# FNet mixing and a cosine-gated MLP: tokens as pairs from folded real DFTs, the channel transform folded into the weights, integer phase rounding

## The chip, the cores and the metric

The kernel runs on one core of one Trainium2 chip. Times are device microseconds (us) from the first to the last instruction of an execution. Several executions are timed and the median is quoted. The engines are TensorE (PE in the profile, PEld for its weight loads), VectorE (DVE), ScalarE (ACT), GpSimd (POOL) and SyncE (SP, which here only issues DMAs). A "record" is one line of the trace: an instruction with its start and duration.

## The reference

```python
def _attn_ref(x):                    # x: (8, 3008, 256) float32
    X = np.fft.fft(x, axis=1)        # over the sequence: "s-DFT", 3008 points
    X = np.fft.fft(X, axis=2)        # over the channels: "d-transform", 256 points
    return X.real.astype(np.float32)

def _moe_ref(x, w_in, w_out):        # x: (24064, 256), w_in: (256, 2048), w_out: (2048, 256)
    h = x @ w_in
    g = h * np.cos(h)
    return (g @ w_out).astype(np.float32)
```

The output is `_moe_ref` of the flattened `_attn_ref`, all in float32.

## The kernel before

3008 is 47 times 64. Stage A does the 47-point factor of the s-DFT as matmuls with a 47-row operand and writes the result to a scratch tensor in DRAM, from which it is read back in another layout. Then six chunks of up to 512 tokens follow per batch: the second DFT factor (`BJ`), the d-transform (`CdS`), the first MLP matmul (`w1`), the phase chain, the second MLP matmul (`w2`).

```python
def emit_A(b, xts):                            # stage A
    zd = zdram_tile()                          # [94, 64 * 256] in DRAM
    for g in range(8):
        sa = stagA_tile()                      # [94, 2048]
        for q in range(4):
            n = 4 * g + q
            pa = pbig_tile()
            nc.tensor.matmul(pa, lhsT=LA, rhs=xts[:, n * 512 : (n + 1) * 512], start=True, stop=True)
            nc.vector.tensor_copy(out=sa[:, q * 512 : (q + 1) * 512], in_=pa[0:94, :])
        nc.sync.dma_start(out=zd[:, g * 2048 : (g + 1) * 2048], in_=sa)
    return zd
# ... emit_chunk: z2 loaded from zd, BJ matmuls, copies, CdS matmuls, copies; then per hidden slice f of 16:
    for cc in range(2):
        nc.tensor.matmul(pm[:, 0:ntok], lhsT=w1[cc][:, f * 128 : (f + 1) * 128], rhs=at[cc][:, 0:ntok],
                         start=(cc == 0), stop=(cc == 1))
    nc.scalar.activation(out=tt, in_=pm, func=AF.Copy, bias=BIG, scale=1.0)           # round to integer
    nc.vector.scalar_tensor_tensor(out=mm, in0=tt, scalar=-BIG, in1=pm, op0=ALU.add, op1=ALU.subtract)
    nc.scalar.activation(out=ss, in_=mm, func=AF.Sin, bias=0.0, scale=-math.pi)       # half angle
    nc.scalar.activation(out=qq, in_=ss, func=AF.Square, bias=0.0, scale=math.sqrt(2.0))
    nc.vector.scalar_tensor_tensor(out=gt, in0=qq, scalar=-1.0, in1=pm, op0=ALU.add, op1=ALU.mult)
    # ... four 128x256 matmuls of slice f - 2 with w2
```

(Shortened: slices of the tile widths and the loop over sub-blocks are left out.)

## Time and profile before

| | before |
|---|---|
| median | 4,835.48 us (4,835.38 to 4,835.50, 4 runs) |
| TensorE busy | 3,646 us, 75% |
| VectorE, ScalarE busy | 1,328 us, 1,523 us |
| mean granted TensorE clock | 0.876 |

The first lines of the page give each engine's busy time, then 40 equal slices of the span: a digit is the busy share in tenths, PEclk the clock granted to TensorE in tenths.

```profile
span 4834.8 us, 30926 instructions
PE 3645.8 (75%) x12000; PEld 2201.5 (46%) x12000; DVE 1328.4 (27%) x1985; ACT 1523.2 (32%) x2594; POOL 150.4 (3%) x196
PE   0408995499863998739977499666995579958998
PEclk9999995799966998769977799677996789959999
DMA  2101101111011010111001110011101021011100
```

An average of 75% hides two regimes: runs of 9 (TensorE is full) and pits. The windows view of five stretches of 30 us shows what they are. Its columns are the stretch, its length, busy us and instruction count of each engine, the granted clock, the mean busy share of the 16 DMA engines, and GB/s.

```profile
170.00:200.00 30.00, 14.38 (x16) 4.79 (x16) 5.32 (x8) 0.00 (x0) 0.00 (x0) 1.00 0.13 54
290.00:320.00 30.00, 0.00 (x0) 0.00 (x0) 0.00 (x0) 0.00 (x0) 0.00 (x0) 1.00 0.07 28
410.00:440.00 30.00, 30.00 (x107) 19.82 (x106) 12.20 (x18) 15.96 (x26) 0.00 (x0) 1.00 0.00 1
740.00:770.00 30.00, 14.38 (x16) 4.79 (x16) 5.32 (x8) 0.00 (x0) 0.00 (x0) 0.50 0.13 53
920.00:950.00 30.00, 0.00 (x0) 0.00 (x0) 0.00 (x0) 0.00 (x0) 0.00 (x0) 0.50 0.06 26
```

Stage A (170, 740) advances at the speed of scratch stores that keep 0.13 of the DMA engines busy, which is 2 of 16. The lower clock at 740 costs nothing: the stage does the same 16 matmul records in 30 us at 1.00 and at 0.50. At 290 and 920 nothing computes; one DMA engine of 16 (0.06 to 0.07) is loading. At 410 TensorE has no gap.

In the list of costliest groups (line, engine, operation, names, shapes, count, then busy us and mean ns, then idle time before it and what ended it) stage A is the matmul L153:

```profile
L153 PE MATMUL pbig<-xbig,LA 47*128 47x512 f32 x512 | 417.1, 982 | 535.6 <-DVE stagA L160 398.6
L160 DVE COPY stagA<-pbig 94x512 f32<-94x512 f32 x256 | 171.0, 685 | 770.7 <-DMA zdram<-stagA 492.5
```

417 us busy plus 536 us idle, and the waits view adds 612 us in which the first `BJ` matmul of a batch waits for the scratch reload (145 us once, 73 to 78 us six times, 17 us once). In all that is about 1,565 us; the rest, about 3,270 us, is TensorE almost without a gap. The timeline there (start, duration, records):

```profile
414.57 1.89 PE L227 MATMUL po<-w_78,gj 128*128 128x256 f32 x8
416.30 1.02 PE L238 MATMUL pm<-at,w_74 128*128 128x512 f32 x2
417.15 1.02 PE L238 MATMUL pm<-at,w_75 128*128 128x512 f32 x2
418.01 1.89 PE L227 MATMUL po<-w_78,gj 128*128 128x256 f32 x8
```

A float32 matmul leaves two records. From 414.57 to 418.01 one hidden slice takes 3.44 us; a 128x512 matmul takes 0.85 us from start to start, a 128x256 one 0.43 us. A record's duration (1.02 for two) is longer than the distance to the next start.

### The profile page before, as it was taken

The page shows a single profiled execution, that of the slowest core. Times are in us where ns is not written, and L with a number is a line of the kernel's source. Part 1 is how long each engine was busy: PE and PEld are TensorE (multiplying, and loading weights), DVE is VectorE, ACT ScalarE, POOL GpSimd, SP SyncE. Part 2 cuts the span into 40 slices and gives each one's busy share as a digit, 9 for nine tenths or more (in the row PEclk, how much of TensorE's full clock was granted, in tenths as well). Part 3 has the DMA queues.
Part 4 walks back from the last instruction along what each step waited for, and adds up shares of the span by engine and source line. Part 5 has one row for each costly group of instructions (what it writes and reads, how often), then busy time and mean ns, then how long its engine had stood idle before and what let it go on. Part 6 is the DMA issues. An engine that isn't in the chain of part 4 may idle for free.

```text
span 4834.8 us, 30926 instructions
## 1 busy us (share of the span) xinstructions
PE 3645.8 (75%) x12000; PEld 2201.5 (46%) x12000; DVE 1328.4 (27%) x1985; ACT 1523.2 (32%) x2594; POOL 150.4 (3%) x196
## 2 busy tenths in 40 slices
PE   0408995499863998739977499666995579958998
PEld 0105662266532664326633366334662356625665
DVE  0102331133321333213322133222332123323333
ACT  0003440144411543214422144122440234503444
POOL 0000000000000000000000000000000000000000
PEclk9999995799966998769977799677996789959999
DMA  2101101111011010111001110011101021011100
GB/s 87 46 31 42 26 6 54 37 33 26 15 50 51 14 26 24 45 47 27 16 29 45 39 27 17 37 40 36 26 17 45 36 43 22 9 53 33 27 17 9
DMA packets 109475, 158.33 MB, mean 33 GB/s; under 512 B 46057, under 2 KB 96280, under 8 KB 102552
## 3 DMA queue, kind: packets, MB, share of 16 engines
q1 hardware_dynamic: 59024, 131.04, 8.9%
q0 software_dynamic: 50304, 25.31, 2.5%
q8 instruction: 94, 1.54, 0.1%
q14 instruction: 53, 0.43, 0.0%
HBM read 81.75 MB, written 73.92 MB: 32 GB/s over the span
## 4 chain that ended last, share of the span: by engine, by line
issue 87%; another core or an unknown queue 5%; PE 3%; POOL 2%; DMA 2%; DVE 0%; ACT 0%; POOLq 0%; SPq 0%; DVEq 0%
POOL out_dram L294 2%; DMA zdram<-stagA 2%; PE po L227 1%; PE pm L238 1%; PE pbig L153 0%; PE pbig L210 0%; PE pbig L187 0%; DMA z_198<-zdram 0%; DVE stagA L160 0%; ACT tt L246 0%; DVE mm L250 0%; POOLq L294 0%; DVE gj L275 0%; ACT L259 0%
## 5 line engine op out<-in xcount | busy, mean ns | idle before, releaser
L227 PE MATMUL po<-w_78,gj 128*128 128x256 f32 (+1 forms) x6144 | 1471.7, 382 | 0.0
L227 PEld LDWEIGHTS po<-w_78,gj 128*128 128x128 f32 (+1 forms) x6144 | 1141.7, 188 | 491.5 <-issue 360.1
L153 PE MATMUL pbig<-xbig,LA 47*128 47x512 f32 x512 | 417.1, 982 | 535.6 <-DVE stagA L160 398.6
L238 PE MATMUL pm<-at,w_74 128*128 128x512 f32 (+1 forms) x1536 | 787.6, 594 | 28.9 <-DVE gj L275 28.9
L250 DVE SCALAR_TENSOR_TENSOR mm<-tt,pm 128x512 f32<-128x512 f32 (+1 forms) x768 | 519.4, 676 | 1004.5 <-ACT tt L246 1004.5
L238 PE MATMUL pm<-at,w_75 128*128 128x512 f32 (+1 forms) x1536 | 777.7, 588 | 0.0
L275 DVE SCALAR_TENSOR_TENSOR gj<-qq,pm 128x512 f32<-128x512 f32 (+1 forms) x768 | 519.2, 676 | 904.8 <-ACT qq L267 904.8
L218 ACT COPY at<-pbig 128x512 f32<-128x512 f32 (+1 forms) x96 | 55.3, 576 | 1962.0 <-PE pbig L210 1962.0
L246 ACT ACTIVATE tt<-pm 128x512 f32<-128x512 f32 (+1 forms) x768 | 450.7, 587 | 682.8 <-PE pm L238 682.8
L259 ACT ACTIVATE ss<-mm 128x512 f32<-128x512 f32 (+1 forms) x768 | 476.5, 620 | 545.0 <-DVE mm L250 545.0
L153 PEld LDWEIGHTS pbig<-xbig,LA 47*128 47x128 f32 x512 | 137.3, 286 | 804.6 <-DVE stagA L160 583.8
L267 ACT ACTIVATE qq<-ss 128x512 f32<-128x512 f32 (+1 forms) x768 | 476.2, 620 | 22.8
L238 PEld LDWEIGHTS pm<-at,w_75 128*128 128x128 f32 x1536 | 288.4, 190 | 362.9 <-issue 332.4
L160 DVE COPY stagA<-pbig 94x512 f32<-94x512 f32 x256 | 171.0, 685 | 770.7 <-DMA zdram<-stagA 492.5
L238 PEld LDWEIGHTS pm<-at,w_74 128*128 128x128 f32 x1536 | 279.5, 190 | 157.2 <-issue 84.3
L195 DVE COPY xt<-pbig 128x512 f32<-128x512 f32 x192 | 127.2, 677 | 788.9 <-PE pbig L187 788.9
L294 POOL DMA_DIRECT2D out_dram<-osb x192 | 150.2, 789 | 4675.2 <-ACT osb L293 4675.0
L210 PE MATMUL pbig<-xt,CdS_70 128*128 128x512 f32 (+1 forms) x384 | 181.2, 594 | 0.7
L210 PE MATMUL pbig<-xt,CdS_71 128*128 128x512 f32 (+1 forms) x384 | 177.0, 583 | 0.0
L187 PE MATMUL pbig<-BJ,z_198 128*128 128x128 f32 x32 | 6.7, 405 | 145.2 <-DMA z_198<-zdram 145.2
L210 PEld LDWEIGHTS pbig<-xt,CdS_71 128*128 128x128 f32 x384 | 73.0, 190 | 88.4 <-issue 88.4
L210 PEld LDWEIGHTS pbig<-xt,CdS_70 128*128 128x128 f32 x384 | 69.0, 190 | 70.9 <-issue 66.3
(103 smaller groups left out, 500.1 us busy)
## 6 DMA issues: line engine op xcount, KB each, us to landing
zdram<-stagA SPq DMA_DIRECT2D x64, 752.0 KB
out_dram<-osb POOLq DMA_DIRECT2D x184, 128.0 KB, 8.4
BJ<-fft_BJ SPq DMA_DIRECT2D x1, 3008.0 KB
w_78<-in_moe_w_out_dram SPq DMA_DIRECT2D x1, 2048.0 KB
w_74<-in_moe_w_in_dram SPq DMA_DIRECT2D x1, 1024.0 KB
w_75<-in_moe_w_in_dram SPq DMA_DIRECT2D x1, 1024.0 KB
z_198<-zdram SPq DMA_DIRECT2D x2, 512.0 KB
z_529<-zdram SPq DMA_DIRECT2D x2, 512.0 KB
```

Source lines behind the costliest of these rows:

```text
L153: nc.tensor.matmul(pa, lhsT=LA, rhs=xts[:, n * 512 : (n + 1) * 512], start=True, stop=True,)
L160: nc.vector.tensor_copy(out=sa[:, q * 512 : (q + 1) * 512], in_=pa[0:94, :])
L195: nc.vector.tensor_copy(out=xt[dch][:, 0 : 2 * ntok] .rearrange("p (hp j k) -> p j hp k", hp=2, j=nj)[:, 4 * g : 4 * g + ng, :, :], in_=pb ...
L210: nc.tensor.matmul(pd[:, 0:ntok], lhsT=CdS[dch][:, ri * 256 + cc * 128 : ri * 256 + cc * 128 + 128], rhs=xt[dch][:, ri * ntok : ri * ntok ...
L227: nc.tensor.matmul(pos[sub][0:nt, 0:ND], lhsT=gts[f][:, t0:t1], rhs=w2[:, f * ND : (f + 1) * ND], start=(f == 0), stop=(f == 15),)
L238: nc.tensor.matmul(pm[:, 0:ntok], lhsT=w1[cc][:, f * 128 : (f + 1) * 128], rhs=at[cc][:, 0:ntok], start=(cc == 0), stop=(cc == 1),)
L246: nc.scalar.activation(out=tt[:, 0:ntok], in_=pm[:, 0:ntok], func=AF.Copy, bias=BIG, scale=1.0)
L250: nc.vector.scalar_tensor_tensor(out=mm[:, 0:ntok], in0=tt[:, 0:ntok], scalar=-BIG, in1=pm[:, 0:ntok], op0=ALU.add, op1=ALU.subtract,)
L259: nc.scalar.activation(out=ss[:, 0:ntok], in_=mm[:, 0:ntok], func=AF.Sin, bias=0.0, scale=-math.pi,)
L267: nc.scalar.activation(out=qq[:, 0:ntok], in_=ss[:, 0:ntok], func=AF.Square, bias=0.0, scale=math.sqrt(2.0),)
L275: nc.vector.scalar_tensor_tensor(out=gt[:, 0:ntok], in0=qq[:, 0:ntok], scalar=-1.0, in1=pm[:, 0:ntok], op0=ALU.add, op1=ALU.mult,)
L294: nc.gpsimd.dma_start(out=out_r[b, 8 * c + t0 // 64 : 8 * c + t1 // 64, :, :], in_=ob[0:nt, :],)
```

## The change

The intent is to need fewer matmul columns and no large scratch tensor (a small one in DRAM stays, for one channel).

- For real input, the real output of token k is R - I and that of token -k is R + I (or the reverse), where R and I are the even and odd parts of the spectrum. So one product with R and one with I gives both tokens: h(k) = P + Q, h(-k) = P - Q, with P = Wc R and Q = Ws I.
- The d-transform is folded into `w_in` once at the start: Wc holds `w_in` combined with cosines, Ws with sines.
- The s-DFT is done on sequences folded twice (x(s) with x(-s), then with the half-length shift), as 24 matmuls of about 376 columns per batch, placed inside the stream of MLP steps. Channel 128 has no room in the 128 rows and goes as an "extra channel", for batches 1 to 7 together, from two DMAs that pick single 4-byte elements.
- The phase is rounded by writing int32 from ScalarE, and the sine is taken directly, which saves the squaring pass.

The stream has 376 steps (47 tiles of 256 token pairs, 8 steps each). The diff, cut to the core of the step (the folding, DFT, output rows and setup are left out):

```diff
-        for f in range(16):
-            pm = pm_tile()
-            for cc in range(2):
-                nc.tensor.matmul(pm[:, 0:ntok], lhsT=w1[cc][:, f * 128 : (f + 1) * 128], ...
+    def mlp1(T, s):                                  # TW = 256
+        for i in range(2):
+            nc.tensor.matmul(pp[:, i * TW : (i + 1) * TW], lhsT=Wc[:, f * 128 : (f + 1) * 128],
+                             rhs=Rr[:, pos : pos + TW], start=True, stop=True)
+        for i in range(2):
+            nc.tensor.matmul(pq[:, i * TW : (i + 1) * TW], lhsT=Ws[:, f * 128 : (f + 1) * 128],
+                             rhs=Ir[:, pos : pos + TW], start=True, stop=True)
+        for i in range(2):                           # extra channel
+            nc.vector.scalar_tensor_tensor(out=pt[...], in0=Rb[:, pos : pos + TW],
+                scalar=wex[:, f : f + 1], in1=pp[...], op0=ALU.mult, op1=ALU.add)
+        nc.vector.tensor_tensor(out=h[:, 0:512], in0=pt, in1=pq, op=ALU.add)
+        nc.vector.tensor_tensor(out=h[:, 512:1024]...[:, :, ::-1], in0=pt..., in1=pq..., op=ALU.subtract)
+        act_chain(h, 1024)
+    def act_chain(h, n):
+        nc.scalar.activation(out=k, in_=h[:, 0:n], func=AF.Copy, bias=0.25, scale=1.0)    # k is int32
+        nc.vector.tensor_tensor(out=r[:, 0:n], in0=h[:, 0:n], in1=k, op=ALU.subtract)
+        nc.scalar.activation(out=r[:, 0:n], in_=r[:, 0:n], func=AF.Sin, bias=halfpi, scale=TWO_PI)
+        nc.vector.tensor_tensor(out=h[:, 0:n], in0=h[:, 0:n], in1=r[:, 0:n], op=ALU.mult)
+    # mlp2, two steps later: 8 matmuls 128x256 of h with w2
+    def load_ext():                                  # 4-byte elements, batches 1 to 7
+        for t, row in ((X0, 0), (X1, SEQ - 1536)):
+            nc.scalar.dma_start(out=t, in_=bass.AP(..., ap=[[SEQ * ND, NB - 1], [ND, 1536], [1, 1]]))
```

So a step has 12 matmuls of 256 columns on TensorE, and on VectorE two 256-wide, two 512-wide and two 1024-wide operations.

## The prediction

> **What bounds it now.** Two regimes alternate, eight times. In the chunks TensorE is the limit: the timeline shows no gap, one 128-wide hidden slice for 512 tokens repeats every 3.445 us, a 128x512 fp32 matmul takes 0.853 us (two records), a 128x256 one 0.431 us, granted clock 1.00. Windows at the s-DFT stage show PE busy 14.4 of 30 us, clock 0.50, DMA share 0.13 at 54 GB/s. The costliest groups give that stage 417 us busy plus 536 us idle (behind VectorE, which waits for the scratch stores, and the first x load); the waits give 612 us more for scratch reloads. So about 1,565 of 4,835 us is DFT through DRAM, about 3,270 saturated TensorE. The slow DMAs fit the Trainium skill, "DMA: Bandwidth & Descriptors", section on why a DMA increments its semaphore by 16: a transfer uses the largest k up to 16 dividing its slowest dimensions; 94 rows give 2 engines (0.13), 47 give 1 (0.06 in this trace).
>
> **Removed.** Scratch round trip and waits (1,565 us, all on the path); d-transform matmuls (384 x 0.853 = 330 us); second DFT factor (about 370 us); half of the first MLP matmul, as one product serves tokens k and -k (1,300 to 650 us).
> **Unchanged.** Second MLP matmul, 3,008 x 0.431 = 1,297 us.
> **Added.** Folded DFT, 24 matmuls of 376 columns (0.63 us) per batch, 121 us; weight folding and extra channel, about 35 us; sums and differences on VectorE.
>
> TensorE after: 376 steps x 12 x 0.431 = 1,946 us, plus DFT: about 2,100 us.
>
> **VectorE becomes nearly equal.** Its 512-wide operation took 0.687 us, its 448-wide 0.621: about 1.04 ns per element plus 0.15 us. The skill's "VectorE: DVE Perf Modes", section on the TRN2 errata, gives (N+151)/0.96 ns for fp32 tensor_tensor, which agrees (691, 624). Estimate per step: 2 x 0.42 (256 wide) + 2 x 0.69 + 2 x 1.22 (1024 wide) = 4.66 us, with folding 5.1. ScalarE: 0.83 ns per element plus 0.2 us, 2.3 us per step. In the scheduled order the phase subtraction follows its own sum closely in two of three steps, so VectorE waits for the rounding copy: by hand three steps take 15.8 us, 5.26 each, against 5.18 for TensorE. With folding and lumps of DFT matmuls I expect 5.75 us, 376 x 5.75 = 2,160 us: two engines bound together, neither saturated.
>
> **Start.** About 10 MB of loads need some 45 us. But the scheduler put folding of the extra channel of batches 1 to 7 (7 rows, 21,504 elements of 4 bytes, probably 7 engines) ahead of batch 0's folding on VectorE. At an estimated 20 to 60 ns each (500 B packets took 38 ns) it lands after 60 to 180 us; the MLP stream starts 50 us later. I take 180 us for the start, 15 for the tail.
>
> **Predicted: 2,360 us; 8 in 10 between 2,220 and 2,570.** Faster by over 2%: 0.98; within: 0.01; slower: 0.01.
>
> **Right would show as:** steps of 5.5 to 6.0 us; PE and VectorE both 85 to 92% busy in the stream, ScalarE near 42%; clock 1.00; VectorE mainly waiting for the rounding copy; before the stream, VectorE waiting for the 4-byte loads; no stall at batch boundaries.
> **Wrong:** int32 subtraction or reversed writes slower than 1.2 and 0.7 us; VectorE operations overlapping so that TensorE alone binds (5.5 us steps, 2,250 us in all); DFT lumps or output stores stalling the stream (over 6.3 us, 2,550); 4-byte loads beyond 250 us.

## The result, and the profile after

| | before | after |
|---|---|---|
| median | 4,835.48 us | 2,210.32 us (2,209.99 to 2,211.21, 4 runs) |
| TensorE busy | 3,646 us, 75% | 2,146 us, 97% |
| VectorE busy | 1,328 us, 27% | 1,817 us, 82% |
| ScalarE busy | 1,523 us, 32% | 904 us, 41% |
| mean granted clock | 0.876 | 0.984 |

The ratio is 0.4572, 95% interval 0.4565 to 0.4578. The result is correct. It is 150 us better than the predicted 2,360, and 10 us below the low end of the range.

The head of the page of the kernel after:

```profile
span 2209.4 us, 24488 instructions
PE 2146.2 (97%) x9640; PEld 1823.4 (83%) x9640; DVE 1816.5 (82%) x2520; ACT 903.9 (41%) x898; POOL 117.3 (5%) x100
PE   3599999999999999999999999999999999999999
DVE  0479989888998879888898889888788887888877
PEclk7699999999999999999999999999999999999999
```

There are no pits. The windows view of the stream in one piece (same columns as above) answers to the window 410:440 of before:

```profile
140.00:2200.00 2060.00, 2059.55 (x9380) 1772.01 (x9379) 1770.86 (x2443) 882.78 (x871) 66.15 (x54) 1.00 0.07 23
```

TensorE is idle for 0.45 of 2,060 us. VectorE is busy 86% and waits for the rest. So TensorE alone sets the pace, and VectorE, which was predicted to bind together with it, fits underneath.

Why it fits is to be seen in VectorE's timeline. VectorE's order mostly repeats every three steps; this is one such cycle, with the first line of the next:

```profile
1441.22 1.23 DVE L496 TENSOR_TENSOR r<-h,r 128x1024 f32<-128x1024 f32 x1
1442.36 0.87 DVE L470 SCALAR_TENSOR_TENSOR pt<-Rb,wex,pp 128x256 f32<-128x256 f32 x2
1443.33 0.69 DVE L479 TENSOR_TENSOR h<-pt,pq 128x512 f32<-128x512 f32 x1
1443.94 1.22 DVE L502 TENSOR_TENSOR h<-h,r 128x1024 f32<-128x1024 f32 x1
1445.08 0.68 DVE L480 TENSOR_TENSOR h<-pt,pq 128x512 f32<-128x512 f32 x1
1446.94 1.23 DVE L496 TENSOR_TENSOR r<-h,r 128x1024 f32<-128x1024 f32 x1 [1.18 <-ACT r L493]
1448.08 0.87 DVE L470 SCALAR_TENSOR_TENSOR pt<-Rb,wex,pp 128x256 f32<-128x256 f32 x2
1449.05 0.69 DVE L479 TENSOR_TENSOR h<-pt,pq 128x512 f32<-128x512 f32 x1
1449.66 1.22 DVE L502 TENSOR_TENSOR h<-h,r 128x1024 f32<-128x1024 f32 x1
1450.79 0.68 DVE L480 TENSOR_TENSOR h<-pt,pq 128x512 f32<-128x512 f32 x1
1452.19 0.48 DVE L470 SCALAR_TENSOR_TENSOR pt<-Rb,wex,pp 128x256 f32<-128x256 f32 x1 [0.72 <-PE pp L451]
1452.65 1.23 DVE L496 TENSOR_TENSOR r<-h,r 128x1024 f32<-128x1024 f32 x1
1453.80 0.47 DVE L470 SCALAR_TENSOR_TENSOR pt<-Rb,wex,pp 128x256 f32<-128x256 f32 x1
1454.38 0.69 DVE L479 TENSOR_TENSOR h<-pt,pq 128x512 f32<-128x512 f32 x1
1454.98 0.68 DVE L480 TENSOR_TENSOR h<-pt,pq 128x512 f32<-128x512 f32 x1
1455.58 1.22 DVE L502 TENSOR_TENSOR h<-h,r 128x1024 f32<-128x1024 f32 x1
1456.84 1.23 DVE L496 TENSOR_TENSOR r<-h,r 128x1024 f32<-128x1024 f32 x1
```

L496 has a record of 1.23 us, but the next operation starts 1.14 us after it. L479 has 0.69 and its successor starts after 0.61. L502 has 1.22, its successor starts after 1.14. Where an operation has nothing to wait for, it starts 0.08 to 0.09 us before the record ahead of it ends. Durations are right for a chain (L479 needs what L470 wrote and starts 0.10 us after the end of its record, at 1443.33) and too long for a sum of what an engine can do. The wait for the rounding copy that the prediction named is there too (1.18 us at L496), and 159 us of it in the whole stream. But the same cycle also has a wait of 0.72 us for TensorE: VectorE is ahead of it.

The start holds the second difference. The matching lines of the timeline before the stream:

```profile
2.18 33.38 ACTq L403 DMA_DIRECT2D Ir<-in_x_dram  x1
35.59 1.28 ACT L210 ACT_TABLE_LOAD   x1 [35.59 <-issue]
39.99 0.15 DVE L417 TENSOR_TENSOR Rb<-Rr 7x1 f32<-7x1 f32 x1 [39.11 <-DMA Rr<-in_x_dram]
66.00 0.93 DVE L416 TENSOR_TENSOR Rb<-Rr,Ir 7x752 f32<-7x752 f32 x1 [24.06 <-DMA Ir<-in_x_dram]
121.22 0.59 PE L451 MATMUL pp<-Rr,Wc 128*128 128x256 f32 x2
```

VectorE stood 39 us and then 24 us behind the two 4-byte loads, as predicted, and merely issuing the second of them held ScalarE for 33 us. The loads landed at 40 and 66 us. SyncE stood behind them too. Its own waits (line, what it waited for, us in total, times, longest):

```profile
SPq L146 <- DMA Rr<-in_x_dram: 36.1, 1, 36.1
SPq L157 <- DMA Ir<-in_x_dram: 24.7, 1, 24.7
```

L146 loads the weights, L157 the DFT matrices: two of the four weight loads were issued only when the first 4-byte load had landed, and seven of the eight matrix loads only when the second had. The stream began in earnest at 121 us, not at 180.

### The profile page after: what moved, and what is told of

Its sections match the earlier page's. It is cut to its first block, busy times and chain, and to the rows that moved or that the text cites. A ratio compares the mean times of both kernels' runs of the same rounds, so it can differ in the third digit from the quotient of the medians.

```text
span 2209.4 us, 24488 instructions
## 1 busy us (share of the span) xinstructions
PE 2146.2 (97%) x9640; PEld 1823.4 (83%) x9640; DVE 1816.5 (82%) x2520; ACT 903.9 (41%) x898; POOL 117.3 (5%) x100
## 3 DMA queue, kind: packets, MB, share of 16 engines
q10 hardware_dynamic: 21518, 0.09, 1.3%
## 4 chain that ended last, share of the span: by engine, by line
PE 94%; issue 3%; POOL 1%; DVE 1%; DMA 0%; ACT 0%; DVEq 0%; ACTq 0%; POOLq 0%
PE pp L451 15%; PE pq L460 15%; PE da L294 3%; PE db L294 3%; POOL xl_327 L129 1%; PE po_4085 L518 1%; PE po_10602 L518 1%; PE po_9324 L518 1%; PE po_7948 L518 1%; PE po_6581 L518 1%; PE po_3838 L518 1%; PE po_7270 L518 1%; PE po_6123 L518 1%; PE po_5905 L518 1%; PE po_5662 L518 1%
## 5 line engine op out<-in xcount | busy, mean ns | idle before, releaser
L493 ACT ACTIVATE r<-h 128x1024 int32<-128x1024 f32 x377 | 397.8, 1055 | 646.6 <-DVE h L480 639.6
L499 ACT ACTIVATE r<-r,halfpi 128x1024 f32<-128x1024 f32 x377 | 432.4, 1147 | 482.9 <-DVE r L496 482.8
L496 DVE TENSOR_TENSOR r<-h,r 128x1024 f32<-128x1024 f32 x377 | 460.4, 1221 | 169.7 <-ACT r L493 164.2
L502 DVE TENSOR_TENSOR h<-h,r 128x1024 f32<-128x1024 f32 x377 | 459.1, 1218 | 37.1 <-ACT r L499 36.3
L451 PE MATMUL pp<-Rr,Wc 128*128 128x256 f32 x1504 | 389.1, 380 | 0.0
L460 PE MATMUL pq<-Ir,Ws 127*128 127x256 f32 x1504 | 388.1, 380 | 0.0
L470 DVE SCALAR_TENSOR_TENSOR pt<-Rb,wex,pp 128x256 f32<-128x256 f32 x752 | 334.8, 475 | 56.0 <-PE pp L451 55.4
L451 PEld LDWEIGHTS pp<-Rr,Wc 128*128 128x128 f32 x1504 | 285.9, 190 | 46.8 <-issue 1.9
L460 PEld LDWEIGHTS pq<-Ir,Ws 127*128 127x128 f32 x1504 | 285.6, 190 | 40.7 <-issue 0.6
L479 DVE TENSOR_TENSOR h<-pt,pq 128x512 f32<-128x512 f32 x376 | 257.7, 685 | 30.1 <-DVE pt L470 0.9
L480 DVE TENSOR_TENSOR h<-pt,pq 128x512 f32<-128x512 f32 x376 | 255.6, 680 | 0.0
```

The costliest lines, as they stand in the source:

```text
L451: nc.tensor.matmul(pp[:, i * TW : (i + 1) * TW], lhsT=Wc[:, f * 128 : (f + 1) * 128], rhs=Rr[:, pos : pos + TW], start=True, stop=True,)
L460: nc.tensor.matmul(pq[:, i * TW : (i + 1) * TW], lhsT=Ws[:, f * 128 : (f + 1) * 128], rhs=Ir[:, pos : pos + TW], start=True, stop=True,)
L470: nc.vector.scalar_tensor_tensor(out=pt[:, i * TW : (i + 1) * TW], in0=Rb[:, pos : pos + TW], scalar=wex[:, f : f + 1], in1=pp[:, i * TW : ...
L479: nc.vector.tensor_tensor(out=h[:, 0:512], in0=pt, in1=pq, op=ALU.add)
L480: nc.vector.tensor_tensor(out=h[:, 512:1024].rearrange("p (f c) -> p f c", f=2)[:, :, ::-1], in0=pt.rearrange("p (f c) -> p f c", f=2), in ...
L493: nc.scalar.activation(out=k, in_=h[:, 0:n], func=AF.Copy, bias=0.25, scale=1.0)
```

## The experiments

Two theories of the stream were set against each other. T: TensorE alone binds, because VectorE's operations overlap at their ends. R: the prediction's, VectorE's ordered loop with its waits for ScalarE binds together with TensorE. The start and the old kernel's slow stage were tested apart. Each kernel derived from the changed one was scheduled anew by the framework, so the order of VectorE's operations can differ a little from one to the other; where this limits a conclusion it is said. The experiments ran in three later sessions, each beside the kernel before, whose median there was 4,833.3 to 4,834.9 us against 4,835.5 in the first; the changed kernel itself was not run again, so differences of one or two us mean nothing.

### The old phase chain in the new kernel

```diff
-        nc.scalar.activation(out=k, in_=h[:, 0:n], func=AF.Copy, bias=0.25, scale=1.0)
-        nc.vector.tensor_tensor(out=r[:, 0:n], in0=h[:, 0:n], in1=k, op=ALU.subtract)
-        nc.scalar.activation(out=r[:, 0:n], in_=r[:, 0:n], func=AF.Sin, bias=halfpi, scale=TWO_PI)
-        nc.vector.tensor_tensor(out=h[:, 0:n], in0=h[:, 0:n], in1=r[:, 0:n], op=ALU.mult)
+        nc.scalar.activation(out=rr, in_=hh, func=AF.Copy, bias=BIG, scale=1.0)
+        nc.vector.scalar_tensor_tensor(out=rr, in0=rr, scalar=-BIG, in1=hh, op0=ALU.add, op1=ALU.subtract)
+        nc.scalar.activation(out=rr, in_=rr, func=AF.Sin, bias=0.0, scale=-math.pi)
+        nc.scalar.activation(out=rr, in_=rr, func=AF.Square, bias=0.0, scale=math.sqrt(2.0))
+        nc.vector.scalar_tensor_tensor(out=hh, in0=rr, scalar=-1.0, in1=hh, op0=ALU.add, op1=ALU.mult)
```

> The changed kernel with the old phase chain (big-number rounding, half-angle sine, square; three ScalarE passes instead of two, the same two VectorE passes). Theory T (TensorE alone binds the stream, the other engines have slack): within 15 us of 2,210. Rival R (the order of VectorE with its waits for ScalarE binds together with TensorE, as predicted): one more 1.06 us pass in that loop costs 0.3 to 1 us per step, plus 110 to 400 us. Correct result.

(The sign of the scale on `w2` is turned as well.) Measured: 2,213.75 us (4 runs), correct; 3.4 us more than the changed kernel. ScalarE's busy time rose from 904 to 1,262 us and nothing came of it. R falls, and the integer rounding, one of the four parts of the change, is worth practically nothing in time: it relieves an engine that does not bind.

### One more matmul per step

```diff
+        nc.tensor.matmul(dps("da")[:, 0:256], lhsT=Wc[:, 0:128], rhs=w2[:, 0:256], start=True, stop=True)
         if s == 7:
             store(T)
```

> One more 128x256 matmul per step (into an unused bank), 376 x 0.431 = 162 us more of TensorE. Theory T: plus 155 to 170 us, about 2,372. Rival R: part hides in TensorE's waits, plus less than 110 us. Correct result.

Measured: 2,383.48 us (2 runs), correct; 173 us more. None of the added 162 us is hidden, so TensorE binds. The 11 us beyond the sum of the matmuls are not explained; TensorE's idle time in the stream is some 4 us instead of 0.5, which is only a part.

### More work for VectorE

```diff
         act_chain(h, 1024)
+        dum = spool.tile([128, 512], FP, tag="dum", bufs=1, name="dum")        # or 1024
+        nc.vector.tensor_tensor(out=dum, in0=w2[:, 0:512], in1=w2[:, 1024 : 1024 + 512], op=ALU.add)
```

> One more 512-wide addition per step on VectorE into a scratch tile (0.60 us start to start, 226 us in all). Correct result. Theory T (VectorE has about 0.9 us of slack per step, part of it as waits): plus 0 to 60 us. Rival R (bound together): plus 150 to 226 us.

> The same with a 1024-wide addition (1.14 us start to start, 429 us in all). Correct result. Theory T: VectorE is now needed 5.4 us plus 0.35 of folding per step, more than TensorE's 5.5, so it shows: plus 90 to 250 us. Rival R: plus 350 to 430 us.

Measured: 2,217.41 us with 512 (plus 7 us) and 2,326.90 us with 1024 (plus 117 us), both correct, 2 runs each. The windows view of the stream with 512 added:

```profile
140.00:2200.00 2060.00, 2060.00 (x9377) 1771.65 (x9376) 1962.27 (x2811) 883.56 (x873) 74.30 (x54) 1.00 0.07 23
```

VectorE went from 1,771 to 1,962 us busy in these 2,060 us and TensorE stayed without a gap; of the 7 us, 6 lie in the start, where the stream began at 127 us. So VectorE had at least 0.6 us of slack per step, and, as the run with 1024 shows, less than 1.14. Summing records would have denied it: 4.75 us per step in the changed kernel plus about 0.4 of folding plus 0.69 is 5.84, above TensorE's 5.5. Summing distances from start to start (about 0.40, 0.60 and 1.14, twice each, 4.28) gives 4.28 + 0.4 + 0.60 = 5.28, below it. (The 0.4 is an estimate: 16 folding operations of 0.86 us from start to start in the trace and the DFT's sums, per batch of 47 steps.)

The run with 1024 tells the two ways of counting apart. There VectorE is busy for 2,146 of the 2,175 us from 140 to 2,315, so it is now the limit. Distances give 4.28 + 0.4 + 1.14 = 5.82 us per step, 0.29 above the 5.53 of the changed kernel, or an estimated 109 us in all; records give 4.75 + 0.4 + 1.22 = 6.37, or 316 us. Measured were 117.

### Less work for TensorE

```diff
                 f = 2 * s + i
+                if i:
+                    continue
                 for gr in range(2):
...
-                        stop=(f == NF - 1),
+                        stop=(f == NF - 2),
```

> Every second hidden slice is left out of the second matmul: 4 of 12 matmuls per step fewer, TensorE 3.45 us plus about 0.28 of DFT per step. Wrong result on purpose. What remains is the rate of the VectorE and ScalarE loop. Theory T (back-to-back VectorE operations start 0.08 to 0.09 us before the record of the one ahead ends, so its step takes 4.3 us plus 0.35 of folding plus some waiting): 4.7 to 5.1 us per step, total 1,890 to 2,050. Rival R (the loop takes 5.26 us plus folding as the prediction had it): within 60 us of 2,210.

Measured: 1,903.16 us (1,899 to 1,907, 2 runs), with a wrong result, as intended. The page's head:

```profile
span 1897.6 us, 18448 instructions
PE 1646.1 (87%) x6632; PEld 1206.2 (64%) x6632; DVE 1774.8 (94%) x2520; ACT 892.6 (47%) x898; POOL 118.0 (6%) x100
```

Now VectorE is the full engine (busy for 1,728 of the 1,750 us from 140 to 1,890), and the stream, which began at 120 us, takes (1,903 - 129) / 376 = 4.7 us per step with its folding included (129 being the start and 9 us of tail). The prediction had 5.26 for the loop alone and 5.75 with folding. The order of VectorE's operations here is not that of the changed kernel (the scheduler mixed more folding between them), so this measures what VectorE can do, not the exact loop of the changed kernel.

### The sharing between k and -k undone

```diff
         for i in range(2):
             f = 2 * s + i
-            nc.tensor.matmul(pp[...], lhsT=Wc[...], rhs=Rr[...], start=True, stop=True)
...
-            nc.tensor.matmul(pq[...], lhsT=Ws[...], rhs=Ir[...], start=True, stop=True)
+            for ps, W in ((pp, Ws), (pq, Wn)):             # Wn = -Ws
+                nc.tensor.matmul(ps[...], lhsT=Wc[...], rhs=Rr[...], start=True, stop=False)
+                nc.tensor.matmul(ps[...], lhsT=W[...], rhs=Ir[...], start=False, stop=True)
...
-        nc.vector.tensor_tensor(out=h[:, 0:512], in0=pt, in1=pq, op=ALU.add)
-        nc.vector.tensor_tensor(out=h[:, 512:1024]... , in0=pt..., in1=pq..., op=ALU.subtract)
+            # the two 256-wide extra-channel operations of each half now write h directly, four per step
```

> Only the sharing of the first matmul between tokens k and -k is undone: both sums are accumulated on TensorE from the cosine weights and the sine weights or their negative, 8 matmuls of 256 columns instead of 4 per step, and VectorE loses its sum and difference (four 256-wide operations of about 0.40 us instead of two and two 512-wide of 0.60). The sine's scale is lowered by 3e-7 so that its argument stays in range. Correct result. Theory T: plus 376 x 4 x 0.431 = 648 us, total 2,830 to 2,900, TensorE saturated, VectorE's 0.4 us less per step worth nothing. Rival R: the lighter VectorE gives part of it back, plus less than 550 us.

Measured: 2,864.91 us (2 runs), correct; 655 us more than the changed kernel. TensorE was without a gap for all 2,710 us from 140 to 2,850, VectorE 62% busy. The sharing is therefore worth its matmuls, 648 us by the sum, and the operations that it adds on VectorE cost nothing.

### The start: loads moved, first try

```diff
-                nc.scalar.dma_start(
+                nc.sync.dma_start(
...
-    if NB > 1:
-        load_ext()
     fold_weights()
...
+        at(2, load_ext)
         at(22, lambda: dft_ext(1, NB - 1, fold_ext()))
```

> The 4-byte loads of the extra channel are issued two steps into the stream, on the SyncE queue, instead of first. Theory (the start is held by them: VectorE waited 39 and 24 us for them and all other loads crawled beside them): the stream starts at 60 to 80 us instead of 121, the total falls by 40 to 60 us to about 2,150 to 2,170. Rival (the other loads and batch 0's folding and DFT need that long anyway): the total changes by less than 15 us. Correct result.

Measured: 2,202.27 us (2,190.81 to 2,204.48, 5 runs), correct; only 8 us less, with an unusual spread (the profiled run is the fastest of the five). By its number the rival would stand. But the trace shows that the experiment did not do what it was for: the framework issued the loads at 32 us, before the stream began, and VectorE still waited 9 and 18 us for them; the first 40 us, now nearly free of 4-byte traffic, went fast (326 and 379 GB/s), and then the same crawl came (10 GB/s between 60 and 80 us). The stream began at 99 us. A part of the cost had moved, not gone.

### The start: loads forced into the stream

```diff
+        def gate(dst, q, s):
+            nc.scalar.copy(out=dst, in_=tiles[q].g[s][0 : NB - 1, 0:1])
+        def gated_load():
+            gate(X0[:, 0:1], 0, 3)
+            gate(X1[:, 0:1], 0, 3)
+            load_ext()
+        # gated_fold: the same for the buffers that the folding writes, with the hidden tile of step 19
+        at(4, gated_load)
+        at(20, lambda: dft_ext(1, NB - 1, gated_fold()))
```

A copy of one column from a hidden tile of step 3 into the target buffer (which the load then overwrites) makes the load depend on a step that really is late. (As in the first try, the early call is gone and SyncE issues the loads.)

> The previous attempt only moved the 4-byte loads to 32 us, still ahead of the stream, and VectorE still stood behind them. Here tiny ScalarE copies from the hidden tiles of step 3 and step 19 into the target buffers force load and folding into the stream. Theory (they hold the start): the stream starts at 60 to 70 us instead of 121, total 2,145 to 2,170 us, and the stream itself stays saturated. Rival (moved into the stream they cost there what they cost at the start, by holding up loads, stores or VectorE): within 15 us of 2,200. Correct result.

Measured: 2,158.29 us (2,157.38 to 2,159.13, 4 runs), correct; ratio to the kernel before 0.4464 (0.4456 to 0.4471), 52 us less than the changed kernel. The windows of the first 40 us and of a stretch with the 4-byte loads, first of the changed kernel, then of this one:

```profile
0.00:20.00 20.00, 6.73 (x8) 2.35 (x8) 0.06 (x1) 0.00 (x0) 11.68 (x16) 1.00 0.82 217
20.00:40.00 20.00, 3.00 (x4) 1.18 (x4) 0.01 (x1) 2.36 (x3) 0.00 (x0) 0.59 0.69 9
```

```profile
0.00:20.00 20.00, 9.09 (x15) 3.76 (x16) 5.81 (x11) 3.04 (x4) 13.89 (x17) 1.00 0.90 328
20.00:40.00 20.00, 20.00 (x84) 15.23 (x83) 9.04 (x14) 3.10 (x6) 16.65 (x11) 0.75 1.04 380
100.00:120.00 20.00, 20.00 (x94) 17.59 (x93) 19.95 (x29) 9.88 (x10) 0.00 (x0) 1.00 0.83 2
```

In the changed kernel the DMA engines are 0.69 busy from 20 to 40 us and move 9 GB/s. What moves is small elements (9,753 packets of their queue and 52 others by the DMA view of these 20 us), while SyncE, which should issue the other loads, waits for the first 4-byte load to land. Forced later, the same loads keep the engines 0.83 busy for 2 GB/s, but TensorE beside them has no gap in these 20 us. The stream begins at 65 us instead of 121. Whether VectorE's wait or SyncE's set the start is not told apart: this version removes both. This version beats both kernels.

### The old kernel with its transfers reshaped

```diff
-        return spool.tile([94, 2048], FP, tag="stagA", bufs=2, name="stagA")
+        return spool.tile([96, 2048], FP, tag="stagA", bufs=2, name="stagA")
-        return dpool.tile([94, 64 * ND], FP, tag="zdram", bufs=2, name="zdram")
+        return dpool.tile([96, 64 * ND], FP, tag="zdram", bufs=2, name="zdram")
-        nc.sync.dma_start(out=t, in_=x_r[b].rearrange("s2 s1 d -> s2 (s1 d)"))
+        src = x_r[b].rearrange("s2 s1 d -> s2 (s1 d)")
+        nc.sync.dma_start(out=t[0:32], in_=src[0:32])
+        nc.sync.dma_start(out=t[32:NJ], in_=src[32:NJ])
-                    out=sa[:, q * 512 : (q + 1) * 512], in_=pa[0:94, :]
+                    out=sa[:, q * 512 : (q + 1) * 512], in_=pa[0:96, :]
```

> The kernel before with only its slow transfers reshaped: scratch of 96 rows instead of 94 (16 DMA engines instead of 2), x load as 32 and 15 rows instead of 47 (16 and 15 engines instead of 1). Theory (the 1,565 us of the s-DFT stage and its waits are the price of 1 or 2 engines): TensorE's 3,270 us plus about 8 x 30 us for the stage, 8 x 12 us of reload waits and a start of 25 us, 3,550 to 3,750 us. Rival (the round trip through DRAM is slow in itself): over 4,300 us. Correct result.

Measured: 3,756.79 us (2 runs), correct, 7 us above the expected range; ratio to the kernel before 0.7771. The head of its page and the stage A group, to be set against those of the kernel before:

```profile
span 3754.0 us, 30927 instructions
PE 3612.3 (96%) x12000; PEld 2186.8 (58%) x12000; DVE 1332.0 (35%) x1985; ACT 1523.2 (41%) x2594; POOL 150.4 (4%) x196
L155 PE MATMUL pbig<-xbig,LA 47*128 47x512 f32 x512 | 402.0, 969 | 71.0 <-DMA xbig<-in_x_dram 43.6
```

Idle time before the stage's matmuls fell from 536 to 71 us with the same instructions. The waits for the reload fell from 612 to 29 us. So 1,078 of the 2,625 us that the change gained were to be had from four small edits: the scratch round trip was slow because of row counts. The 94 rows of the scratch and the 47 of the x load were changed together, so what each of them cost is not told apart. The other 1,547 us need the new algorithm.

## Why the prediction was right or wrong

**What bounds the kernel before: right.** Two regimes, 1,565 us of stage A and its waits and 3,270 us of full TensorE. The reshaped kernel confirmed the reading of the row counts, though part of what the prediction calls waiting for reloads seems to be the x load. The Trainium skill, "DMA: Bandwidth & Descriptors", section "Why a DMA increments its semaphore by 16 and not by 1", says that a transfer uses the largest number of engines up to 16 that divides its slowest dimensions; this case agrees: 94 rows kept a share of 0.13 busy, 47 rows 0.06, and 96 rows or 32 plus 15 rows took the waits away.

**What the change removes and adds on TensorE: right.** The prediction's sum of 1,946 us for the steps plus DFT, about 2,100 us in all, stands against 2,146 us busy. Undoing the sharing cost 655 us where 650 was the prediction. That the folded d-transform and the second DFT factor are worth their 330 and 370 us is argued from matmul times, not tested alone.

**"I expect 5.75 us per step ... two engines bound together, neither saturated": wrong, and the largest error.** From 121 us to the last stage of the pipeline near 2,200 us the 376 steps took about 5.53 us each: TensorE's own 5.18 us plus its DFT matmuls, with no gap. (5.75 - 5.53) x 376 is 83 us. The step that failed is "by hand three steps take 15.8 us, 5.26 each", a VectorE loop longer than TensorE's step, with the folding then put on top of it. The durations that went into it were nearly right: measured 0.475 against 0.42 for the 256-wide operation, 0.685 against 0.69, 1.22 as assumed, and 1.06 and 1.15 on ScalarE. But they were laid end to end, and operations without a wait start 0.08 to 0.09 us before the record ahead of them ends. The cycle shown above took 15.62 us (1441.22 to 1456.84), which is TensorE's pace (3 x 5.18 = 15.5), and 0.72 of it is the wait for TensorE: without it three steps would take an estimated 14.9 us, 4.97 each, below TensorE's 5.18. With a third of TensorE's matmuls taken away the loop ran at 4.7 us per step, folding included. And the folding costs nothing on top in the changed kernel, because VectorE had room for it: with it, it was still idle for 289 of the 2,060 us. The prediction had named this outcome among its ways to be wrong ("VectorE operations overlapping so that TensorE alone binds, 5.5 us steps, 2,250 us in all") and gave it too little weight; the range should have reached down to TensorE's own sum.

**"I take 180 us for the start": the 4-byte loads did hold it, the size off by about 59 us.** VectorE waited for them and the stream began 55 us after they landed (50 predicted); that SyncE stood behind them too was not foreseen. They landed at 66 us: for 21,504 elements on the seven engines that the prediction assumed this is an estimated 21 ns each, the low end of its 20 to 60 ns, and it took the middle. The seven engines are not confirmed. The share of 0.69 from 20 to 40 us is 11 engines or more than one packet at a time on each, and the queue's 9,753 packets in these 20 us would be 14 ns each on seven engines (an estimate too); few packets moved at first (1,451 of 21,518 in the first 15 us). That the mean duration of a packet in the trace is 21 ns as well (21,518 packets in 1.3% of 16 engines' span) is therefore no confirmation.

**Tail: 15 us predicted, about 9 measured**, from the last multiplication on VectorE near 2,201 us to the end.

The three terms, 83 + 59 + 6, make up the 150 us within 2 us; all three erred to the same side.

**Signs listed in advance.** Steps of 5.5 to 6.0 us (5.53, at the low end), clock 1.00 in the stream, ScalarE near 42% (43%), VectorE between 85 and 92% (86%), its main wait the rounding copy (159 us), no stall at batch boundaries: all seen. PE 85 to 92%: not seen, it was 100%, and this is the sign that tells the two theories apart. Reversed writes and the int32 operand cost nothing extra: 0.68 us for the reversed difference against 0.685 for the plain sum, and 1.22 us with the int32 operand as without.

## What to carry to other kernels

To find out whether an engine has slack, add the distances between starts of back-to-back operations, not their durations, and test it with a dose: a useless operation of a chosen width in every step tells more than any sum. Look at the row counts of slow transfers before rewriting an algorithm; here more than a fifth of the old time lay in 94 and 47 rows. Keep loads of single elements out of the start, and when a scheduler pulls them forward, give them a real dependency on late data.

## What the Trainium skill lacked or had wrong

- "VectorE: DVE Perf Modes", sections "The TRN2 errata — SBUF-src ops pay a fixed extra latency per instruction" and "The DRAIN you can't avoid": the formula (N+151)/0.96 ns gives the records well (691 and 1,224 ns for 512 and 1024; 685 and 1,220 measured), but it is not the cost of one more operation in a row. Starts were 0.60 to 0.61 and 1.14 us apart, 0.08 to 0.09 us less, and 0.5 us per step of this kernel. The page says in passing that an operation which is not held starts earlier, without a figure. The skill as a whole does not lack one: "Vector Engine (DVE) Microarchitecture Reference", section "5.2 Measured stream behaviour on trn2 (trn3 not measured)", has a fixed cost per instruction after overlap. The prediction did not use it.
- "DMA: Bandwidth & Descriptors", section "Why small descriptors are slow (HBM only)": no figure for loads of 4-byte elements. Here two loads of 10,752 such elements each, issued first, landed at 40 and 66 us (21,518 packets, 21 ns each on average, several at a time); forced into the stream, their queue moved 9,856 packets in 20 us.
- The same page, section "Issuing engines are not separate DMA queues": it calls the sequencer's time to initiate a DMA usually small relative to the DMA. For the second of the two loads of 10,752 elements, issuing took 33.4 us of the 64 us from issue to landing and kept ScalarE from its first instruction until 35.6 us; the first, of the same size and with no such load ahead of it, took 1.4 us to issue.
